# The second normalised tiles of block 0: turned by VectorE through DRAM in place of TensorE

## The chip, the cores and the metric

One core of a Trainium2 chip runs the kernel alone. The metric is the device time of one execution in microseconds, the median of repeated runs. The profile is of one further execution on the same kind of core.

## The reference

A transformer block whose two normalisations are scaled and shifted by a condition c. `x` has 2048 rows of 512, `wqkv` is 512 x 1536, the inner width F is 1792, and there are 32 heads of 16.

```python
mod = (_silu(c) @ w_mod).reshape(c.shape[0], 6, 1, -1)
h = _layernorm(x) * (1 + ca) + sa
# attention without softmax: phi(t) = where(t > 0, t + 1, exp(t)) + 1e-6
kv = einsum("bhsd,bhse->bhde", phi(k), v);  z = einsum("bhsd->bhd", phi(k))
o = einsum("bhqd,bhde->bhqe", phi(q), kv) / (einsum("bhqd,bhd->bhq", phi(q), z) + 1e-6)
x = x + ga * (o @ wo)
h = _layernorm(x) * (1 + cb) + sb
x = x + gb * (mish(h @ w1 + b1) @ w2)
```

All of it is float32.

## The kernel before

The 2048 rows are four blocks (b) of 512, a block is four row tiles (t) of 128, and a row of 512 is four column tiles (j) of 128. Every matmul operand is split into a high and a low part (`split`: ScalarE copies the high part, VectorE subtracts it to get the low one), and a product is three matmuls (`mm3`: L76, L77, L78).

The work has stages. First keys and the sums over all rows; then queries, by `q_unit(b, g)` and `q_sevens`; then the output of attention, by `o_unit(b, t)`, twelve matmuls each; then the two dense layers, first for the blocks 0 and 1 and then for 2 and 3. The first dense layer takes two blocks at a time by a seven-product scheme (`pair_begin`, `pair_early`, ..., `product` L1142): its operands are, for each pair of blocks, the second normalised tiles turned so that the 512 columns lie on partitions (`hf`, split as b11, b12, b21, b22) and sums of them (`columns`, t1 to t4).

The order of the instructions is written out by hand. A unit of matmuls is issued in the program's text; what follows it on other engines is a generator given to `spawn`. `tick()` advances every running generator by one `yield`, so a generator's step stands between two units of matmuls, and "one tick earlier" means behind the unit before. `spawn_idle` puts a generator in a list of which the first two are advanced by each tick. Each engine runs its own instructions in order; so do the DMA queues of SP and POOL with the issuing of transfers. SBUF tiles come from one pool of 101 equal buffers (`SLOTS`), PSUM from three pools: "acc" with 4 banks, "h" with 3, "tp" with 1.

The steps around the change are these.

- `attend(b, wait, queue)`: TensorE's denominators `den` of block b (L893), VectorE's reciprocal `rden` (L897, L898), a store of it to DRAM (L900) and four loads that broadcast it to the 16 rows of each head (`rd`, L904), all on the given queue; then, `wait` ticks later, VectorE multiplies the four q tiles by it (L912), and they are split into `qs`, which `o_unit` reads. Block 2 and block 3 use SP.
- `o_post` (L924): VectorE adds the residual to an o unit's PSUM, giving `r`; for the blocks 2 and 3 POOL stores it (`x1d`, L929).
- `norm_first(t)` and `norm_each(b, t)`: mean and variance of a row tile of block 0 or block 1 by two ScalarE passes (`act_sums`) or by VectorE (`ln_stats`), the root by POOL (L207), and the normalised tile `n` by ScalarE (L216).
- `transpose_f(b, j)`: four TensorE transposes of the tiles of column j into one PSUM bank (`tp_n`, L997), and ScalarE scales and shifts them into `hf` (L999).
- `turn(...)`: another way to the same, used for block 3 of the first normalisation (`y_x`) and for the blocks 2 and 3 of the second. POOL stores the normalised row tiles to DRAM (`to_dram`, L247); `load_squares` loads each column tile in four transfers on SP (L262), so that 32 x 32 squares stand at the place of their mirror image; VectorE transposes inside the squares (L267), and ScalarE scales and shifts (L269).
- `w2_job(f)`: scales a tile of w2 (L719), splits it and stores it three times (L729, L731). `rows(g, wait)` loads w1 tiles (`w1p`, L786) and forms their sums and splits (`early_rows` are the first two); `store_rows` stores those (L818).

The lists in the loop at the end of attention give the unit behind which each column tile is turned:

```python
order = {8: [(0, 0), (0, 2)], 9: [(0, 1)], 10: [(0, 3), (1, 0)], 11: [(1, 2)], 12: [(1, 1)], 13: [(1, 3)]}
```

Of the kernel before, what the change touches and what calls it, by code (L numbers as in the profile page):

```python
# [27 lines left out]
def block_kernel(ctx: ExitStack, tc: tile.TileContext, x, wqkv, wo, w1, b1t, w2, c, wmodt, out):  # L28
# [23 lines left out]
    def spawn(gen):  # L52
        fresh.append(iter(gen))

    def spawn_idle(gen):

        idle_work.append(gen)

    def tick():

        running.extend(fresh)
        fresh.clear()
        for g in list(running):
            if next(g, "end") == "end":
                running.remove(g)
        for g in idle_work[:width[0]]:
            if next(g, "end") == "end":
                idle_work.remove(g)
# [145 lines left out]
    def ln_apply(key, b, j, t, dst, engine):  # L214
        if engine is act:
            act.activation(dst, t, AF.Identity, bias=nb[key, b][:, j:j + 1], scale=rs[key, b][:, j:j + 1])  # L216
        else:
            engine.tensor_scalar(dst, t, mv[key, b][:, j, 0:1], rs[key, b][:, j:j + 1],
                                 op0=ALU.subtract, op1=ALU.mult)
# [143 lines left out]
    def q_unit(b, g):  # L363
        p = ps("h", f"pq_{b}_{g}")
        gs = slice(P * g, P * (g + 1))
        for k in range(4):
            mm3(p, [w[:, gs] for w in wq[k]], hT["x", b, k], k == 0, k == 3)
        pq[b, g] = sb(f"q_{b}_{g}")
        spawn(phi(p, f"q_{b}_{g}", pq[b, g]))
# [342 lines left out]
    def w2_job(f, wait=2):  # L712
        if f not in w2r:
            load_w2(f)
        if f > 1:
            for _ in range(wait):
                yield
        t = w2r[f]
        dve.tensor_tensor(t, t, bc["gb"], op=ALU.mult)  # L719
        yield  # L720
        yield from split(f"w2_{f}", t, w2s, f)
        yield
        g, n = f // 2, f % 2
        if n == 0:
            w2f[g] = drp.tile([P, 2, D], F32, name=f"w2f_{g}")
            for i in range(2):
                w2d[g, i] = drp.tile([P, 2, D], F32R, name=f"w2d_{g}_{i}")
        for i in range(2):
            pool.dma_start(w2d[g, i][:, n, :], w2s[f][i])  # L729
        if g < KEPT:  # L730
            pool.dma_start(w2f[g][:, n, :], t)  # L731
# [49 lines left out]
    def rows(g, wait):  # L781

        r = [sb(f"w1p_{g}_{i}", F32, (P, 4, P)) for i in range(2)]
        for i in range(2):
            f = 2 * g + i
            sp.dma_start(r[i], w1[:, P * f:P * (f + 1)].rearrange("(k p) f -> p k f", p=P))  # L786
        for _ in range(wait):
            yield
        a11, a12, a21, a22 = [r[i][:, 2 * k:2 * k + 2, :] for i in range(2) for k in range(2)]
        s12, s34 = [sb(f"s{n}_{g}", F32, (P, 4, P)) for n in (12, 34)]  # L790
        s1, s2, s3, s4 = s12[:, 0:2, :], s12[:, 2:4, :], s34[:, 0:2, :], s34[:, 2:4, :]
        dve.tensor_tensor(s1, a21, a22, op=ALU.add)
        dve.tensor_tensor(s2, s1, a11, op=ALU.subtract)
        dve.tensor_tensor(s3, a11, a21, op=ALU.subtract)
        dve.tensor_tensor(s4, a12, s2, op=ALU.subtract)
        yield
        keep, todo = {}, []
        op_rows[g] = keep
        for name, v, parts in (("a1", r[0], ("a11", "a12")), ("s12", s12, ("s1", "s2")), ("s34", s34, ("s3", "s4")),
                               ("a22", a22, ("a22",))):  # L800
            half = split(f"{name}_{g}", v, keep, name)
            next(half)
            todo.append((name, half, parts))
            if len(todo) == 2:
                yield
                for name, half, parts in todo:
                    run(half)
                    for i, part in enumerate(parts):
                        op_a[g, part] = [h[:, 2 * i:2 * i + 2, :] for h in keep[name]]
                todo = []  # L810
# [19 lines left out]
    early_rows = [rows(g, 3 * g + 1) for g in range(2)]  # L830
# [54 lines left out]
            tick()  # L885


    def attend(b, wait, queue=pool):

        p = ps("tp", f"den_{b}")[:, 0:P]  # L890
        for g in range(4):
            for t in range(4):
                pe.matmul(p[32 * t:32 * (t + 1), :], hmask[:, g, :], pq[b, g][:, P * t:P * (t + 1)],  # L893
                          start=g == 0, stop=g == 3)
        yield
        rden = cst.tile([P, P], F32, tag="rden", name=f"rden_{b}", bufs=2)
        dve.tensor_scalar(rden, p, tiny_den[:, 0:1], 1.0, op0=ALU.add, op1=ALU.mult)  # L897
        dve.reciprocal(rden, rden)  # L898
        d = drp.tile([32, 512], F32, name=f"rden_d_{b}")
        queue.dma_start(bass.AP(tensor=d.tensor, offset=d.offset, ap=[[P, 4], [512, 32], [1, P]]), rden)  # L900
        rd = []
        for g in range(4):
            r = sb(f"rd_{b}_{g}")
            queue.dma_start(r, bass.AP(tensor=d.tensor, offset=d.offset + 8 * g * 512,  # L904
                                     ap=[[512, 8], [0, 16], [1, 512]]))
            rd.append(r)
        for _ in range(wait):
            yield
        parts = []
        for g in range(4):  # L910
            t = pq[b, g]
            dve.scalar_tensor_tensor(t, t, TINY, rd[g], op0=ALU.add, op1=ALU.mult)  # L912
            parts.append(split(f"qs_{b}_{g}", t, qs, (b, g)))
            next(parts[-1])
            if g % 2:
                yield
                run(parts.pop(0))
                run(parts.pop(0))
# [18 lines left out]

    def norm_first(t):

        yield  # L940
        sums = act_sums("n", 0, t, xt["r", 0, t])
        yield
        sums_eps("n", 0, t, sums)
        yield
        sums_shift("n", 0, t, sums)
        yield
        v = xt["n", 0, t] = sb(f"n_0_{t}")
        ln_apply("n", 0, t, xt["r", 0, t], v, act)

    def norm_each(b, t):  # L950

        if t < 2:
            yield
            sums = act_sums("n", b, t, xt["r", b, t])
            yield
            sums_eps("n", b, t, sums)
            yield
            sums_shift("n", b, t, sums)
        else:
            ln_stats("n", b, t, xt["r", b, t])  # L960
            ln_eps("n", b, t, t + 1)
            ln_rstd("n", b, t, t + 1)
            yield
            ln_shift("n", b, t, t + 1)
        v = xt["n", b, t] = sb(f"n_{b}_{t}")
        ln_apply("n", b, t, xt["r", b, t], v, act)
# [27 lines left out]
    def transpose_f(b, j, ptag="tp"):  # L994
        p = ps(ptag, f"tp_n_{b}_{j}")
        for t in range(4):
            pe.transpose(p[:, P * t:P * (t + 1)], xt["n", b, t][:, P * j:P * (j + 1)], ident)  # L997
        hf[b, j] = sb(f"hf_n_{b}_{j}")
        act.activation(hf[b, j], p, AF.Identity, bias=mc[:, 12 + j:13 + j], scale=mc[:, 16 + j:17 + j])  # L999

    def split_b(b, j, name):
        return split(f"{name}_{b}_{j}", hf[b, j], op_b, (name, j % 2))
# [65 lines left out]
        tick()  # L1068
    for g in range(4):
        q_unit(3, g)  # L1070
        tick()
        if g == 1:
            spawn_idle(early_rows[1])
            for t in range(4):
                o_unit(0, t)
                spawn(norm_first(t))
                if t == 1:
                    spawn(attend(2, 5, sp))
                tick()
    act.preload_act_table_set("mish")  # L1080

    order = {8: [(0, 0), (0, 2)], 9: [(0, 1)], 10: [(0, 3), (1, 0)], 11: [(1, 2)], 12: [(1, 1)], 13: [(1, 3)]}
    for b in range(1, NB):
        for t in range(4):
            n = 4 * b + t
            for i, j in order.get(n, ()):
                transpose_f(i, j, "h")
                spawn(split_b(i, j, f"b{j // 2 + 1}{i + 1}"))
            if n in (12, 13):
                spawn(columns(0, n - 12, ("b11", "b12", "b21", "b22")))  # L1090
            if n == 14:
                break
            o_unit(b, t)
            if b == 1:
                spawn(norm_each(1, t))
            if n == 4:
                load_w2(0)
                load_w2(1)
            if n == 5:
                spawn(attend(3, 3, sp))  # L1100
            if n == 7:
                spawn(w2_job(0))
                spawn(w2_job(1))
            tick()


# [163 lines left out]
    for t in (2, 3):  # L1270
        if t == 3:
            spawn(rows(2, 3))
        o_unit(NB - 1, t)
        tick()
    tiles = [norm_tile(b, t) for b in (2, 3) for t in range(4)]
# [279 lines left out]
```

## Time and profile before

| | |
|---|---|
| median of 3 runs | 484.92 us (484.68 to 484.94) |
| profiled execution | 484.99 us, of which the span is 483.0 us |
| instructions | 7291 |
| TensorE, VectorE, ScalarE, POOL busy | 477.7, 384.5, 295.7, 148.4 us |
| granted TensorE clock | 1.00 |
| moved by DMA | 101.69 MB, mean 211 GB/s |

The span is the time from the first to the last instruction in the trace. In the lines that follow, PE is TensorE's matmuls, PEld its weight loads, DVE VectorE, ACT ScalarE, POOL GpSimd and SP the engine that only issues DMAs (SPq). A line of a timeline has its start in us from the start of the span, its length in us, the engine, the line of the kernel, the operation, the tiles written and read, the shape, how many instructions are merged in it and, in brackets, how long the engine stood idle before and what ended that.

### The profile page before, as it was taken

To read this page: it belongs to the slowest core of one execution; us is meant where nothing else is said; L and a number is where in the kernel's file an instruction comes from. 1 tells how busy PE (TensorE), PEld (TensorE's weight loads), DVE (VectorE), ACT (ScalarE), POOL (GpSimd) and SP (SyncE) were. 2 spreads that over 40 slices of the span, in tenths; PEclk is the share of its full clock that TensorE was granted. 3 is DMA by queue.
4 is the path that set the end of the run, shared out by engine and by line. 5 is a ranking of instruction groups with operands and counts; after the bars stand their busy time and mean duration, and the time that the engine had idled before them with its cause. 6 is when DMAs were issued, how large, how long until landed. Compare 5 with 4: busy or idle time off the path is not lost.

```text
span 483.0 us, 7291 instructions
## 1 busy us (share of the span) xinstructions
PE 477.7 (99%) x2342; PEld 393.6 (81%) x2342; DVE 384.5 (80%) x741; ACT 295.7 (61%) x528; POOL 148.4 (31%) x248
## 2 busy tenths in 40 slices
PE   8999999999999999999999999999999999999997
PEld 6788887878878888888888888888888888888887
DVE  7989989999799699977775874899644664789993
ACT  6777686866555979647676755683174454668300
POOL 4583320000022114102324434323617410243500
PEclk9999999999999999999999999999999999999999
DMA  8805599144874307389699998979999922499977
GB/s 312 299 9 127 138 160 266 51 135 150 290 196 110 121 30 263 111 284 335 216 299 350 364 251 187 321 227 340 346 363 332 291 61 62 109 181 211 240 117 167
DMA packets 121823, 101.69 MB, mean 211 GB/s; under 512 B 65937, under 2 KB 87449, under 8 KB 121786
## 3 DMA queue, kind: packets, MB, share of 16 engines
q1 hardware_dynamic: 90504, 55.47, 41.2%
q0 software_dynamic: 29024, 45.24, 37.3%
q10 hardware_dynamic: 2258, 0.53, 0.5%
q8 instruction: 18, 0.29, 0.3%
q14 instruction: 19, 0.16, 0.1%
HBM read 64.50 MB, written 34.61 MB: 205 GB/s over the span
## 4 chain that ended last, share of the span: by engine, by line
PE 93%; DVE 4%; ACT 1%; issue 1%; POOL 0%; ACTq 0%; DVEq 0%
PE p_a L1142 20%; PE p_s L1142 8%; PE oacc L78 5%; PE oacc L76 5%; PE oacc L77 5%; PE m L78 5%; PE m L77 5%; PE m L76 5%; PE o L76 3%; PE o L78 3%; PE o L77 3%; PE pq_a L409 3%; PE pk L78 2%; PE pk L76 2%; PE pk L77 2%; PE gacc L77 2%
## 5 line engine op out<-in xcount | busy, mean ns | idle before, releaser
L207 POOL TENSOR_TENSOR rs_n<-rs_n,half 128x1 f32<-128x1 f32 x16 | 11.4, 711 | 62.0 <-DVE rs_n L202 36.4
L1147 DVE TENSOR_TENSOR cb<-p_s,u 128x512 f32<-128x512 f32 x28 | 19.2, 687 | 11.6 <-ACT u L1183 10.9
L1152 ACT ACTIVATE u<-p_a 128x512 f32<-128x512 f32 x14 | 8.4, 598 | 26.2 <-PE p_a L1142 17.9
L1440 POOL DMA_DIRECT2D wt_m<-w2t x20 | 14.0, 702 | 32.9 <-PE p_a L1142 21.4
L1134 ACT ACTIVATE ub<-cb,b1c 128x512 f32<-128x512 f32 x28 | 20.0, 717 | 5.6 <-DVE cb L1147 5.4
L1177 ACT ACTIVATE u<-p_a 128x512 f32<-128x512 f32 x12 | 7.2, 599 | 24.7 <-PE p_a L1142 24.7
L1183 ACT ACTIVATE u<-p_a 128x512 f32<-128x512 f32 x14 | 8.4, 597 | 15.7 <-PE p_a L1142 15.7
L1147 DVE TENSOR_TENSOR c<-p_a,u 128x512 f32<-128x512 f32 x14 | 9.5, 688 | 8.2 <-PE p_a L1142 7.1
L900 POOL DMA_DIRECT2D rden_d<-rden x2 | 1.4, 719 | 46.5 <-DVE rden L898 46.5
L300 ACT ACTIVATE e_k<-pk 128x512 f32<-128x512 f32 x15 | 8.9, 591 | 10.8 <-PE pk L78 10.8
L779 POOL DMA_DIRECT2D w2b<-w2d x20 | 10.6, 541 | 14.5 <-DVE r L1126 4.6
L773 POOL DMA_DIRECT2D wb<-w2d x14 | 9.9, 709 | 12.4 <-DVE t L751 10.7
L303 DVE SCALAR_TENSOR_TENSOR ku<-e_k,relu_k 128x512 f32<-128x512 f32 x15 | 10.7, 713 | 3.1 <-ACT relu_k L301 3.1
L1111 ACT ACTIVATE u<-p_a,b1c 128x512 f32<-128x512 f32 x14 | 9.6, 684 | 5.4 <-PE p_a L1142 5.4
L303 DVE SCALAR_TENSOR_TENSOR q<-e_q,relu_q 128x512 f32<-128x512 f32 x16 | 10.7, 687 | 2.7 <-ACT relu_q L301 2.7
L207 POOL TENSOR_TENSOR rs_x<-rs_x,half 128x1 f32<-128x1 f32 (+1 forms) x10 | 7.7, 780 | 15.8 <-DVE rs_x L202 14.6
L312 POOL DMA_DIRECT2D ku<-ku x8 | 7.2, 898 | 16.5 <-DVE ku L303 16.5
L826 POOL DMA_DIRECT2D a1b<-rd_a x10 | 5.4, 540 | 21.1 <-DVE b_1l L90 9.6
L924 DVE TENSOR_TENSOR r<-o,r 128x512 f32<-128x512 f32 x16 | 10.9, 680 | 0.9 <-PE o L78 0.9
L719 DVE TENSOR_TENSOR w2r<-w2r,gb_bc 128x512 f32<-128x512 f32 x14 | 9.1, 686 | 2.7 <-DMA w2r<-in_w_dram 2.7
L912 DVE SCALAR_TENSOR_TENSOR q<-q,rd 128x512 f32<-128x512 f32 x16 | 10.5, 689 | 0.5 <-DMA rd<-rden_d 0.5
L929 POOL DMA_DIRECT2D x1d<-r x8 | 4.4, 546 | 20.9 <-DVE r L924 20.9
(1617 smaller groups left out, 1892.6 us busy)
## 6 DMA issues: line engine op xcount, KB each, us to landing
wm<-in_wmodt_dram SPq DMA_DIRECT2D x24, 256.0 KB, 5.4
w2b<-w2d POOLq DMA_DIRECT2D x20, 256.0 KB, 6.3
wt_m<-w2t POOLq DMA_DIRECT2D x20, 256.0 KB, 6.0
r<-in_x_dram SPq DMA_DIRECT2D x16, 256.0 KB, 3.5
x<-in_x_dram SPq DMA_DIRECT2D x15, 256.0 KB, 4.8
w1p<-in_w_dram SPq DMA_DIRECT2D x14, 256.0 KB, 4.1
w2r<-in_w_dram SPq DMA_DIRECT2D x14, 256.0 KB, 6.2
wb<-w2d POOLq DMA_DIRECT2D x14, 256.0 KB, 5.4
```

What stands on the lines that cost most here:

```text
L76: pe.matmul(o, st[0], mv[0], start=start, stop=False)
L77: pe.matmul(o, st[0], mv[1], start=False, stop=False)
L78: pe.matmul(o, st[1], mv[0], start=False, stop=stop)
L207: pool.tensor_tensor(y, y, half[:, lo:hi], op=ALU.pow)
L303: dve.scalar_tensor_tensor(dst, e, 1.0, r, op0=ALU.min, op1=ALU.add)
L409: pe.matmul(p, l, r, start=onto is None and c == 0 and i == 0, stop=c == 1 and i == 2, skip_group_check=onto is not None)
L779: pool.dma_start(w2s[f][i], w2d[f // 2, i][:, f % 2, :])
L924: dve.tensor_tensor(r, p, r, op=ALU.add)
L1134: act.activation(u, p, AF.Mish, bias=b1c[:, f:f + 1])
L1142: pe.matmul(p, st, mv, start=onto is None and c == 0 and i == 0, stop=c == 1 and i == 2, skip_group_check=onto is not None)
L1147: dve.tensor_tensor(out, p, u, op=ALU.add)
L1440: pool.dma_start(v, w2t[g][:, :, SUM[name], :])
```

## The change

Block 0's second normalised tiles go the way of `turn`: each of the four row tiles is stored to DRAM, the column tiles are loaded in sixteen transfers, transposed by VectorE and scaled by ScalarE. TensorE's sixteen transposes of block 0 are gone; block 1's stay. Around that, steps move:

- `norm_first` of the last row tile begins one tick earlier, and the sums of the second pair of w1 tiles are begun one tick earlier.
- `attend(2)` waits four ticks in place of five. `attend(3)` is spawned one unit earlier and waits one tick more.
- The squares of the column tiles 0 and 2 are loaded before unit 5; those of 1 and 3 between the store of block 3's `rden` and the loads of `rd`, on the same queue.
- `order` changes: block 0's splits come one unit or so later, block 1's column tiles 0 and 2 are transposed together behind the same unit.
- In block 1, the row tile 2 takes its statistics from ScalarE.
- The first two `w2_job` go from unit 7 to the last o unit of block 3, behind the first products of the dense layer.

```diff
-    def attend(b, wait, queue=pool):
+    def attend(b, wait, queue=pool, between=None):
...
         queue.dma_start(bass.AP(tensor=d.tensor, offset=d.offset, ap=[[P, 4], [512, 32], [1, P]]), rden)
+        if between is not None:
+            between()
...
     def norm_first(t):
 
-        yield
+        if t < 3:
+            yield
...
         ln_apply("n", 0, t, xt["r", 0, t], v, act)
+        to_dram("n", 0, t, v)
 
     def norm_each(b, t):
 
-        if t < 2:
-            yield
+        if t != 3:
+            if t < 2:
+                yield
             sums = act_sums("n", b, t, xt["r", b, t])
...
     for g in range(4):
         q_unit(3, g)
-        tick()
         if g == 1:
             spawn_idle(early_rows[1])
+        tick()
+        if g == 1:
             for t in range(4):
                 o_unit(0, t)
                 spawn(norm_first(t))
                 if t == 1:
-                    spawn(attend(2, 5, sp))
+                    spawn(attend(2, 4, sp))
                 tick()
...
-    order = {8: [(0, 0), (0, 2)], 9: [(0, 1)], 10: [(0, 3), (1, 0)], 11: [(1, 2)], 12: [(1, 1)], 13: [(1, 3)]}
+    turns = {7: (0,), 8: (2,), 9: (1, 3)}
+    order = {9: [(0, 0)], 10: [(0, 2), (0, 1)], 11: [(0, 3), (1, 0), (1, 2)], 12: [(1, 1)], 13: [(1, 3)]}
     for b in range(1, NB):
         for t in range(4):
             n = 4 * b + t
             for i, j in order.get(n, ()):
-                transpose_f(i, j, "h")
+                if i:
+                    transpose_f(i, j, "h")
                 spawn(split_b(i, j, f"b{j // 2 + 1}{i + 1}"))
+            if n == 5:
+                load_squares("n", 0, (0, 2))
+            for j in turns.get(n, ()):
+                spawn(turn_f(0, j))
...
-            if n == 5:
-                spawn(attend(3, 3, sp))
-            if n == 7:
-                spawn(w2_job(0))
-                spawn(w2_job(1))
+            if n == 4:
+                spawn(attend(3, 4, sp, lambda: load_squares("n", 0, (1, 3))))
             tick()
...
     for t in (2, 3):
         if t == 3:
             spawn(rows(2, 3))
+            spawn(w2_job(0))
+            spawn(w2_job(1))
         o_unit(NB - 1, t)
         tick()
```

More of the change, by code (lines that the diff above doesn't have):

```diff
@@ L1070, in block_kernel @@
         q_unit(3, g)
+        if g == 1:
+            spawn_idle(early_rows[1])
         tick()
         if g == 1:
-            spawn_idle(early_rows[1])
             for t in range(4):
```

## The prediction

> **What bounds the kernel now.** I read the page first: its busy line and its chain of work that ended last.
>
> ```profile
> span 483.0 us, 7291 instructions
> ...
> PE 477.7 (99%) x2342; PEld 393.6 (81%) x2342; DVE 384.5 (80%) x741; ACT 295.7 (61%) x528; POOL 148.4 (31%) x248
> ...
> PE 93%; DVE 4%; ACT 1%; issue 1%; POOL 0%; ACTq 0%; DVEq 0%
> ```
>
> TensorE is busy for 99% and carries 93% of the chain. So a microsecond taken out of TensorE's stream is worth a microsecond, and a microsecond for which TensorE is made to wait is lost at the end, since nothing behind it has slack. Next I read the windows around the change (columns: length, then busy time of PE, PEld, DVE, ACT, POOL, the granted clock, the DMA share and GB/s).
>
> ```profile
> 176.00:183.00 7.00, 7.00 (x38) 5.89 (x38) 6.79 (x19) 4.50 (x9) 2.43 (x3) 1.00 0.23 80
> 183.00:190.00 7.00, 7.00 (x38) 5.88 (x38) 6.82 (x12) 7.00 (x13) 4.32 (x8) 1.00 0.88 299
> 190.00:197.40 7.40, 7.40 (x39) 6.10 (x38) 7.37 (x13) 6.95 (x12) 1.08 (x2) 1.00 0.40 149
> 210.00:222.00 12.00, 12.00 (x55) 9.94 (x54) 7.67 (x15) 6.37 (x12) 0.73 (x2) 1.00 1.00 359
> ```
>
> TensorE never waits here, but VectorE is as full: 6.79 of 7.00, 6.82 of 7.00, 7.37 of 7.40 us. Anything that makes VectorE stand still in this stretch is passed on. At 210 to 222 us the DMA engines are full as well (share 1.00, 359 GB/s).
>
> **What the removed transposes are worth.** The timeline of TensorE at two groups of them (start, length):
>
> ```profile
> 177.40 1.03 PE L997 MATMUL tp_n<-ident,n 128*128 128x128 f32 x8
> ...
> 178.51 0.40 PE L77 MATMUL o<-m_0l,qs_0h 128*128 128x512 f32 x1
> 178.74 0.39 PE L78 MATMUL o<-m_0h,qs_0l 128*128 128x512 f32 x1
> ...
> 191.35 0.48 PE L76 MATMUL o<-m_0h,qs_0h 128*128 128x512 f32 x1
> ...
> 194.21 0.60 PE L997 MATMUL tp_n<-ident,n 128*128 128x128 f32 x4
> ```
>
> Matmuls follow each other every 0.23 us (178.51 to 178.74). From the first transpose to the second matmul behind it pass 178.51 - 177.40 = 1.11 us, where one matmul alone would take 0.23: 0.88 us for 8 transposes, 0.11 each. Block 0 has 16 of them, so the change takes 16 x 0.11 = 1.76 us out of TensorE. ScalarE's four evictions stay as four activations of the same size; the sixteen 128-row pieces are replaced by four DMAs to DRAM, sixteen square loads and four VectorE transposes.
>
> Here a rule differs from the row. The Trainium skill, page "TensorE: Matmul & The Clock Gate", section "Part 4: PE-mode transpose", gives about 275 ns for one transpose in a kernel's context. By that the removal would be worth an estimated 4.4 us and the forecast below would read 486.0 instead of 488.6. The trace has eight overlapped ones in 1.03 us and a step of 0.11, so the measurement decides.
>
> **What VectorE gets.** Four transposes, and it loses the two multiplies and two subtractions of the first two w2 jobs, which go to a later stretch, and one set of statistics.
>
> ```profile
> 71.80 1.30 DVE L267 STREAM_TRANSPOSE hf_x<-y_x 128x512 f32<-128x512 f32 x2
> ...
> 187.79 0.68 DVE L90 TENSOR_TENSOR qs_0l<-q,qs_0h 128x512 fp32r<-128x512 f32 x1
> 188.39 0.69 DVE L90 TENSOR_TENSOR qs_1l<-q,qs_1h 128x512 fp32r<-128x512 f32 x1
> ```
>
> A transpose takes a step of 1.30/2 = 0.65 us, an elementwise operation 0.60 (187.79 to 188.39). Four of the first (2.6) against four of the second (2.4): nothing in sum. What matters is where VectorE must wait.
>
> **The new queue on SP.** In the kernel before, the reciprocal denominators of block 3 go out and come back through SP alone: one store, then four broadcast loads. In the changed kernel the order on SP is: eight square loads (tiles 0 and 2), the store, eight square loads (tiles 1 and 3), then the four broadcasts. Every square reads columns of all four row tiles, so the first waits for the landing of the last tile's write, and behind that wait stand the store and the broadcasts.
>
> ```profile
> 62.13 9.32 SPq L262 DMA_DIRECT2D y_x<-xd  x16
> ...
> 176.58 0.57 SPq L900 DMA_DIRECT2D rden_d<-rden  x1
> 179.09 2.57 SPq L904 DMA_DIRECT2D rd<-rden_d  x4
> ...
> 184.11 0.69 DVE L912 SCALAR_TENSOR_TENSOR q<-q,rd 128x512 f32<-128x512 f32 x1 [0.18 <-DMA rd<-rden_d]
> ...
> 165.98 0.59 ACT L301 ACTIVATE relu_q<-pq 128x512 f32<-128x512 f32 x1
> 166.45 0.63 ACT L84 ACTIVATE a_1h<-w1p 128x512 fp32r<-128x512 f32 x1
> ...
> 167.62 1.28 ACT L1080 ACT_TABLE_LOAD   x1
> ...
> 171.87 0.80 ACT L216 ACTIVATE n<-r,nb_n,rs_n 128x512 f32<-128x512 f32 x1
> 172.57 0.62 ACT L228 ACTIVATE scrap_n<-r 128x512 f32<-128x512 f32 x1
> ...
> 188.43 1.43 ACT L999 ACTIVATE hf_n<-tp_n,mc 128x512 f32<-128x512 f32 x2
> 189.75 0.63 ACT L84 ACTIVATE qs_2h<-q 128x512 fp32r<-128x512 f32 x1
> 190.31 0.63 ACT L84 ACTIVATE qs_3h<-q 128x512 fp32r<-128x512 f32 x1
> ```
>
> When does the last row tile exist? On ScalarE the new order behind relu_q (165.98, done with its step at 166.45) is two splits, the table load, two splits of q, then the row tiles 2 and 3. In the rows two full-width splits lie between 166.45 and 167.62, 1.17 us; in the new pair the second is half as wide, so I take 0.9. Then 1.28 for the table, 2 x 0.56 for the q splits (189.75 to 190.31), 0.70 for tile 2 (171.87 to 172.57) and 0.80 for tile 3: 171.2. Its write then has to land:
>
> ```profile
> L929 POOL DMA_DIRECT2D x1d<-r x8: 539/539/594, 183.6 to 211.3; - x8
> ...
> DMA to landing us min/median/max: 2.3/2.8/4.3
> ```
>
> With the quiet end of that row, 2.3 us, for a write of the same size and queue: 173.5 (with 4.3, 175.5). Eight squares at 9.32/16 = 0.58 us: 178.2. Store, 0.6: 178.8. Eight more squares: 183.5. So the first broadcast is issued at 183.5 instead of 179.09, 4.4 us later, though the store itself is ready early (its matmuls come one unit sooner, see below). In the kernel before the second broadcast ended a wait of VectorE at 184.11; 4.4 us later is 188.5.
>
> VectorE in the new order: q1 at 188.5 (step 0.60), two transposes (1.30), r, then qs_0l from 191.0 to 191.7, qs_1l to 192.3, q2, q3 (to 193.5), one b_0l, r, qs_2l to 195.3, qs_3l to 195.9. TensorE would start o(3,0) at 191.35 - 1.76 + 0.2 = 189.8. Its third matmul needs qs_0l: it arrives at 190.35 and waits until 191.7, 1.35 us. The seventh needs ScalarE's qs_2h (q2 done 192.9, plus 0.6): 0.9 us of waiting. The ninth needs qs_2l at 195.3: 1.35 us. Together 3.6 us, where the kernel before waited for nothing.
>
> Next late is the fourth group of block 1's transposes, tile 3. It takes the PSUM bank ("h", three of them) of the first group, which ScalarE must have evicted. In the new order that eviction (0.7, from the pair at 188.43) stands behind qs_2h and qs_3h (to 194.1), two scalings of turned tiles (2 x 0.7) and two splits (2 x 0.56): 196.6 to 197.3, while TensorE is there at 196.2. Another 1.1 us.
>
> **The earlier denominators.** The den matmuls of block 3 move from behind the second o unit of block 1 to behind the first, and VectorE's last phi of q_3, which they read, now stands behind two products that wait for block 2's broadcasts. Queued behind the wait on TensorE is all its later work.
>
> ```profile
> 161.15 2.64 SPq L904 DMA_DIRECT2D rd<-rden_d  x4
> ...
> 166.60 0.69 DVE L303 SCALAR_TENSOR_TENSOR q<-e_q,relu_q 128x512 f32<-128x512 f32 x1 [1.84 <-ACT relu_q L301]
> ...
> 170.81 1.08 PE L893 MATMUL den<-q,hmask 128*32 128x128 f32 x32
> ```
>
> TensorE would come to them one unit (twelve steps of 0.23, 2.7 us) sooner, at 168.1, and to the last four of them a quarter of a microsecond later. Block 2's second broadcast is issued at 161.8 (161.15 plus a quarter of 2.64), and with the 4.4 us that block 3's took (179.73 to 184.11) it lands at 166.2; q1 and q_3 behind it need 0.60 + 0.69, which is 167.5, or 168.5 where ScalarE's splits in front of them are late. I take 0.2 us; the bounds are 0 (as at 166.60 in the row) and 1.5 (the writes of row tiles 0 and 1, 0.52 MB at 359 GB/s, travel first). The o units that exchange places with den cost the same in either place: nothing.
>
> **The later w2 jobs.** The two jobs leave four VectorE operations, two ScalarE ones and six POOL writes of 256 KB to the stretch after 205 us.
>
> ```profile
> 209.26 1.00 SPq L786 DMA_DIRECT2D w1p<-in_w_dram  x2
> 210.31 0.50 SPq L818 DMA_DIRECT2D rd_a<-a_0h  x1
> ...
> 221.47 0.91 SPq L710 DMA_DIRECT2D w2r<-in_w_dram  x2
> ...
> 214.55 0.69 DVE L1147 TENSOR_TENSOR cb<-p_s,u 128x512 f32<-128x512 f32 x1 [3.51 <-ACT u L1183]
> ...
> 232.60 1.29 DVE L719 TENSOR_TENSOR w2r<-w2r,gb_bc 128x512 f32<-128x512 f32 x2
> ...
> L710 SPq DMA_DIRECT2D w2r<-in_w_dram x14: 328/406/1268, 163.8 to 277.3; - x14
> ...
> DMA to landing us min/median/max: 3.3/5.5/7.5
> ```
>
> In the changed program the buffers come round differently: the second w1p load of row pair 3 waits for the add cb of L1147, which in the trace starts at 214.55, plus the 3.1 us by which all is late by now, plus its 0.69: 218.3 instead of 209.8. Behind it on SP stand sixteen stores (210.31 to 221.47, 11.2 us) and the w2r loads: 229.5, and up to 4.4 us later if the six extra writes (1.57 MB at 359 GB/s) go first. The multiply that reads them is due at 232.60 + 3.1 = 235.7. Landing 3.3 to 5.5 us after the issue gives 232.8 to 239.4, so VectorE waits 0 to 3.7 us, of which TensorE sees what VectorE's own idle time behind it (3.5 us at 214.55, for one) does not take. I take 0.5, bounds 0 and 2.5.
>
> **Sum.** The profiled execution took 484.99 us, 1.99 around its span of 483.0, against a median of 484.92: the same. 484.99 - 1.76 + 0.2 + 3.6 + 1.1 + 0.5 = 488.63, so 488.6.
>
> **Rivals.**
> - *No stall, faster.* If the squares went out at the pace of their quickest issue and the broadcasts landed as before, TensorE would keep only the gain: 484.99 - 1.76 + 0.2 = 483.4. It decides at the second broadcast's landing: at 187.1 or sooner TensorE's first wait is gone, and the others shrink by as much.
>
> ```profile
> L262 SPq DMA_DIRECT2D y_x<-xd x16: 333/487/957, 62.1 to 71.0; - x16
> ```
>
> For it: the quickest issue is 333 ns. Against it: the median is 487 and the whole took 9.32 us; sixteen at 0.33 would save 4.0 us, just what is needed. Chance 0.13, and 0.04 more for a partial stall that ends within 0.2% of before.
> - *Late w2 loads as well.* The chain through the w1p buffer takes its whole 3.7 us and little of it is covered: another 2 to 3 us, 491. For it: the DMA share of 1.00 at 210 to 222 us. Against it: VectorE's idle times. Chance 0.2.
> - *Slow squares.* Each square costs 0.15 us more than the mean of the sixteen (they reach 957 ns in the row): 16 x 0.15 = 2.4 us on the path to the broadcasts, 491.0. For it: they now share the DMA engines with the writes of block 0 and 2. Against it: the sixteen of the row had a full window too. Chance 0.03. The Trainium skill, page "DMA: Bandwidth & Descriptors", section "Specifications", speaks for this one: it wants 512 B or more per transfer for the full rate, and these rows are of 128 B; at a quarter of its 358 GB/s, 1 MB would take an estimated 11.7 us. The trace disagrees by its 9.32 us for the same sixteen.
> - *Dear transposes.* Were each worth its own length (0.60 for four that step by 0.11, so 0.27) and not the step, 16 x 0.16 = 2.6 us less, 486.0. Against it: the steps of these very instructions. Chance 0.02.
>
> **How the numbers follow.** Forecast 0.58, no stall 0.13, partial 0.04, late loads too 0.20, slow squares 0.03, dear transposes 0.02. A measurement of this kernel tells 0.2%, about 1 us, from no change. Slower 0.83, same 0.04, faster 0.13. The forecast's own bounds: squares at the median of 487 ns (16 x 0.09 = 1.4 us) and no w2 wait (0.5) take it down to 486.7, a write that lands in 4.3 us up to 490.6. The range leaves out the fast rival and the far end of the late one: 485.2 to 491.2.
>
> **What would show it.** Right: 16 fewer transposes; VectorE idle for some 4 us before a q product at L914, ended by a broadcast's DMA; TensorE waits in o(3,0) for qs of VectorE and ScalarE, and at the last tp_n group for ScalarE; w1p and the stores on SP some 8 us later. Wrong: TensorE without waits between 185 and 200 us, or a first broadcast issued before 181.

## The result, and the profile after

The changed kernel takes 492.75 us (median of six runs, 492.12 to 493.28) beside 484.85 us of the kernel before (six runs, 484.64 to 484.94): the ratio is 1.0164, interval 1.0151 to 1.0177. It is slower, as forecast, but by 7.9 us where 3.7 were forecast, and 492.75 lies above the range's end of 491.2. The profiled execution took 493.25 us.

The page of the kernel after, its busy line and its chain of work that ended last:

```profile
span 491.5 us, 7306 instructions
...
PE 481.5 (98%) x2326; PEld 393.9 (80%) x2326; DVE 386.2 (79%) x743; ACT 297.4 (61%) x532; POOL 149.8 (30%) x252
...
PE 83%; DVE 8%; DMA 3%; ACT 2%; issue 1%; SPq 1%; POOL 1%; ACTq 0%; DVEq 0%
```

The sixteen transposes are gone (2342 to 2326 matmul instructions), yet TensorE is busy for 3.8 us more. Its share of the last chain fell from 93% to 83%; VectorE and the DMA engines took it. The windows of the kernel after (columns as in the prediction: length, busy PE, PEld, DVE, ACT, POOL, granted clock, DMA share, GB/s) say where:

```profile
183.00:190.00 7.00, 7.00 (x38) 5.69 (x37) 0.69 (x1) 1.40 (x3) 0.58 (x1) 1.00 0.71 175
190.00:200.00 10.00, 6.31 (x15) 3.64 (x16) 9.05 (x15) 6.82 (x12) 1.08 (x2) 0.66 0.28 94
200.00:210.00 10.00, 10.00 (x40) 8.18 (x39) 9.38 (x17) 6.95 (x14) 1.35 (x3) 0.83 0.28 88
```

VectorE does 0.69 us of work in 7 us (183 to 190), where it did 6.82. Then TensorE is idle for 3.7 of 10 us, and the granted clock is 0.66 and 0.83. That is why TensorE's busy time grew: the same matmuls took longer. The timelines of the kernel after, of SP's issuing and then of VectorE:

```profile
174.40 4.04 SPq L262 DMA_DIRECT2D y_n<-nd  x8
178.54 0.58 SPq L900 DMA_DIRECT2D rden_d<-rden  x1
179.22 5.19 SPq L262 DMA_DIRECT2D y_n<-nd  x8
184.51 2.57 SPq L906 DMA_DIRECT2D rd<-rden_d  x4
```

```profile
188.55 0.69 DVE L914 SCALAR_TENSOR_TENSOR q<-q,rd 128x512 f32<-128x512 f32 x1 [5.69 <-DMA rd<-rden_d]
190.73 0.69 DVE L914 SCALAR_TENSOR_TENSOR q<-q,rd 128x512 f32<-128x512 f32 x1 [1.49 <-DMA rd<-rden_d]
191.34 1.30 DVE L267 STREAM_TRANSPOSE hf_n<-y_n 128x512 f32<-128x512 f32 x2
...
193.13 0.67 DVE L90 TENSOR_TENSOR qs_0l<-q,qs_0h 128x512 fp32r<-128x512 f32 x1
```

And TensorE, first in the kernel before and then in the kernel after, at the second, third and ninth matmul of o(3,0) and at the first product of the dense layer (in brackets the idle time and what ended it):

```profile
191.67 0.40 PE L77 MATMUL o<-m_0l,qs_0h 128*128 128x512 f32 x1
191.90 0.40 PE L78 MATMUL o<-m_0h,qs_0l 128*128 128x512 f32 x1
...
193.29 0.40 PE L78 MATMUL o<-m_2h,qs_2l 128*128 128x512 f32 x1
...
197.40 0.39 PE L1142 MATMUL p_a<-b_0h,a_0h 128*128 128x512 f32 x1
```

```profile
190.29 0.40 PE L77 MATMUL o<-m_0l,qs_0h 128*128 128x512 f32 x1
193.86 0.79 PE L78 MATMUL o<-m_0h,qs_0l 128*128 128x512 f32 x1 [3.17 <-DVE qs_0l L90]
194.45 0.63 PE L76 MATMUL o<-m_1h,qs_1h 128*128 128x512 f32 x1
...
197.46 0.80 PE L78 MATMUL o<-m_2h,qs_2l 128*128 128x512 f32 x1 [0.52 <-DVE qs_2l L90]
...
203.34 0.43 PE L77 MATMUL o<-m_2l,qs_2h 128*128 128x512 f32 x1
...
204.52 0.39 PE L1152 MATMUL p_a<-b_0h,a_0h 128*128 128x512 f32 x1
```

The difference of the starts is the running account. TensorE comes to o(3,0) 1.38 us ahead (190.29 against 191.67). At the third matmul it is 1.96 behind: the step there took 3.57 us instead of 0.23. At the ninth it is 4.17 behind, at p_a 7.12. Between 193.86 and 203.34 neighbouring matmuls start about 0.43 us apart where they had 0.23. The span ends 8.5 later, so another 1.4 is lost behind p_a.

### The profile page after: what moved, and what is told of

Same layout as the page of the kernel before. It is cut to its first block, busy times and chain, and to the rows that moved or that the text cites. A ratio compares the mean times of both kernels' runs of the same rounds, so it can differ in the third digit from the quotient of the medians.

```text
span 491.5 us, 7306 instructions
## 1 busy us (share of the span) xinstructions
PE 481.5 (98%) x2326; PEld 393.9 (80%) x2326; DVE 386.2 (79%) x743; ACT 297.4 (61%) x532; POOL 149.8 (30%) x252
## 4 chain that ended last, share of the span: by engine, by line
PE 83%; DVE 8%; DMA 3%; ACT 2%; issue 1%; SPq 1%; POOL 1%; ACTq 0%; DVEq 0%
PE p_a L1152 19%; PE p_s L1152 8%; PE oacc L76 5%; PE oacc L78 5%; PE oacc L77 5%; PE m L77 5%; PE m L76 5%; PE m L78 5%; PE pq_a L409 3%; PE pk L76 2%; PE pk L78 2%; PE pk L77 2%; PE gacc L77 2%; PE gacc L78 2%; PE gacc L76 2%; PE o L78 2%
## 5 line engine op out<-in xcount | busy, mean ns | idle before, releaser
L914 DVE SCALAR_TENSOR_TENSOR q<-q,rd 128x512 f32<-128x512 f32 x16 | 10.4, 683 | 7.2 <-DMA rd<-rden_d 7.2
L826 POOL DMA_DIRECT2D a1b<-rd_a x10 | 5.4, 540 | 24.3 <-PE p_a L1152 11.1
L269 ACT ACTIVATE hf_n<-hf_n,mc 128x512 f32<-128x512 f32 x12 | 9.3, 804 | 4.3 <-DVE hf_n L267 4.3
```

## The experiments

The theory after the result (A): the late broadcasts make TensorE wait for over 3 us, the wait lowers its clock, and both cost time. The rivals are named in the expectations. The first four kernels of the table ran on one chip beside the kernel before, and so did the next four, the four after them, and the last. From group to group the kernel before varies by 0.3 us.

| kernel | median us | before us | ratio, interval |
|---|---|---|---|
| fill14 | 494.56 | 484.90 | 1.0202 (1.0187 to 1.0217) |
| rd_first | 495.45 | 484.90 | 1.0224 (1.0203 to 1.0245) |
| rd_pool | 492.82 | 484.90 | 1.0164 (1.0149 to 1.0180) |
| w2_back | 491.69 | 484.90 | 1.0151 (1.0132 to 1.0170) |
| fill14_w2 | 491.76 | 485.14 | 1.0139 (1.0099 to 1.0180) |
| fill14_early | 495.70 | 485.14 | 1.0208 (1.0172 to 1.0244) |
| turn11 | 490.07 | 485.14 | 1.0095 (1.0066 to 1.0124) |
| turn11_w2 | 493.37 | 485.14 | 1.0158 (1.0139 to 1.0177) |
| before_late8 | 490.24 | 485.12 | 1.0111 (1.0079 to 1.0143) |
| before_late16 | 494.41 | 485.12 | 1.0204 (1.0178 to 1.0230) |
| order4 | 486.86 | 485.12 | 1.0039 (1.0024 to 1.0054) |
| order4_mid | 486.03 | 485.12 | 1.0015 (1.0002 to 1.0029) |
| order4_mid13 | 485.40 | 485.04 | 1.000 (0.999 to 1.001) |

### fill14: TensorE kept busy during the wait

```diff
+                fill = ps("tp", "fill")
+                for _ in range(14):        # between the second and the third matmul of o(3,0)
+                    pe.matmul(fill, q[0], ms[g][0], start=True, stop=True)
```

> The changed kernel with 14 extra matmuls into a PSUM bank that nobody reads, put between the second and the third matmul of o(3,0), where TensorE stood still for 3.3 us (14 x 0.23 = 3.2 us). Theory A (standing still for over 3 us is what lowered the granted clock to 0.66): the third matmul still starts at about 193.9, but it and those behind it step by 0.23 instead of 0.43; the ninth waits for qs_2l until 197.4 all the same, and behind it 16 steps and four transposes take 4.1 us instead of 7.1: 2.9 us less, 489.8. Rival B (the clock falls from load or from the broadcasts, not from the wait): the drop is still there, 492.7, within 0.5.

Timeline of TensorE in this kernel, and its window:

```profile
190.11 3.36 PE L943 MATMUL fill<-m_0h,qs_0h 128*128 128x512 f32 x14
...
196.38 0.50 PE L78 MATMUL o<-m_2h,qs_2l 128*128 128x512 f32 x1 [1.01 <-DVE qs_2l L90]
198.36 0.66 PE L1011 MATMUL tp_n<-ident,n 128*128 128x128 f32 x4 [0.79 <-ACT hf_n L1013]
201.60 0.39 PE L1161 MATMUL p_a<-b_0h,a_0h 128*128 128x512 f32 x1
...
246.02 0.50 PE L1161 MATMUL p_s<-b_2h,s_2h 128*128 128x512 f32 x1 [2.93 <-DVE cb L1166]
```

```profile
190.00:200.00 10.00, 7.93 (x35) 5.67 (x34) 9.30 (x16) 7.90 (x14) 1.62 (x3) 1.00 0.22 83
```

With TensorE busy through the stall the clock stays at 1.00 here, so in this stretch it was the standing still that lowered it, and not the load or the broadcasts (rival B). Two later kernels with the same 14 matmuls limit this; they follow below. From the ninth matmul to p_a pass 5.22 us instead of 7.06; by these two profiled executions the low clock cost 1.84. It is not 2.9, because at full clock TensorE meets the wait that the prediction had at the last tp_n group (0.79 and the slower restart). The other 1.08 by which p_a is sooner came from broadcasts that happened to land sooner. And yet the number was missed, and the whole is 1.8 us slower than the changed kernel: everything won is lost again at 246 us, and more, at a wait of 2.93 us for cb (the longest for cb in the changed kernel is 0.7). A second chain ends there.

### rd_first and rd_pool: the broadcasts sooner

```diff
# rd_first                                   # rd_pool
-        if between is not None:             -  spawn(attend(3, 4, sp, lambda: ...))
-            between()                       +  spawn(attend(3, 4, pool, lambda: ...))
         rd = []
...
             rd.append(r)
+        if between is not None:
+            between()
```

> The changed kernel with the four broadcast loads of block 3 ahead of the second eight square loads on SP instead of behind them. Theory A (the broadcasts were late because of the queue): first broadcast issued at about 179.2, its q product at 183 to 184; the transposes of tiles 1 and 3 then wait for their squares (to about 189), qs_0l at 191, TensorE waits 0.5 us at the third matmul of o(3,0) and about 2 at the ninth, the clock stays at 1.00: 487.4 (485.5 to 489). Rival C (the four transposes and VectorE's order are what is late, whatever the broadcasts do): the wait at the third matmul stays over 3 us and the time is 492 or more.

> The changed kernel with block 3's store of the denominators and its four broadcasts on POOL's queue, the sixteen squares alone on SP. Theory A: broadcasts issued at about 176.5 and landed by 182, squares landed by 186.3, qs_0l at 189.2, no wait at the third matmul, 0.9 us at the ninth, clock 1.00: the first product p_a of the last stage starts 0.5 us sooner than in the kernel before, and with the 1.2 us lost to the later w2 jobs the time is 485.5 (484 to 487). Rival C (transposes and VectorE's order): 491 or more. Rival D (POOL's queue delivers the broadcasts no sooner than SP's): 490 to 493, with q products again at 188 or later.

The timelines of SP and of VectorE in rd_first, and then the same two of rd_pool:

```profile
180.98 2.55 SPq L904 DMA_DIRECT2D rd<-rden_d  x4
183.58 8.16 SPq L262 DMA_DIRECT2D y_n<-nd  x8
```

```profile
186.50 0.69 DVE L914 SCALAR_TENSOR_TENSOR q<-q,rd 128x512 f32<-128x512 f32 x1 [1.08 <-DMA rd<-rden_d]
192.30 0.71 DVE L267 STREAM_TRANSPOSE hf_n<-y_n 128x512 f32<-128x512 f32 x1 [5.10 <-DMA y_n<-nd]
```

```profile
175.70 13.93 SPq L262 DMA_DIRECT2D y_n<-nd  x16
```

```profile
190.60 0.71 DVE L267 STREAM_TRANSPOSE hf_n<-y_n 128x512 f32<-128x512 f32 x1 [2.51 <-DMA y_n<-nd]
```

Both missed their numbers (487.4 and 485.5) and lie where rival C put them (492 or more, 491 or more). The second q product came 4.2 us sooner in rd_first and 3.3 in rd_pool, but now VectorE waits for squares, and TensorE waits 5.25 and 1.89 us for qs_0l. Behind the broadcasts eight squares take 8.16 us to issue, 1.02 each, where the first eight of the changed kernel took 4.04; beside the broadcasts of the other queue sixteen take 13.93. Whichever goes first, the other is late, and VectorE's order asks for both before qs_0l. So the trade is not on SP's queue alone: broadcasts in flight slow the squares. Rival C is right that VectorE's order of transposes matters, but what makes it late is the squares, and not the transposes' own time.

### w2_back, fill14_w2, fill14_early: the second chain

```diff
# w2_back, and with the 14 matmuls fill14_w2    # fill14_early (with the 14 matmuls)
+            if n == 7:                          +            load_w2(4)
+                spawn(w2_job(0))                +            load_w2(5)
+                spawn(w2_job(1))                             store_rows(0)
...
     for t in (2, 3):
         if t == 3:
             spawn(rows(2, 3))
-            spawn(w2_job(0))
-            spawn(w2_job(1))
```

> The changed kernel with the first two w2 jobs back behind unit 7, where the kernel before has them. Theory A (the later w2 jobs cost 0.4 and 0.8 us at two products behind 210 us): 1.2 us less, 491.5; the wait in o(3,0) is unchanged, since the four VectorE operations fall into the 5.7 us in which VectorE waits for the broadcast. Rival E (their six writes travel with the broadcasts and make them later, as the prediction's order of costs did not say): the wait in o(3,0) grows by 1 us or more and the time is 493 to 495.

> The 14 extra matmuls and the first two w2 jobs back behind unit 7. Theory F (two chains end close together: the stall in o(3,0), and the late loads w2r of jobs 4 and 5, which stand on SP behind sixteen stores and a w1p load and are due near 242 us; whoever shortens the first alone waits for the second): with the w2 jobs early the loads are out by 230 and the wait of 2.9 us for cb at 246 with its own drop of the clock is gone, so 490.6 to 491.7, some 3 to 4 us less than with the 14 matmuls alone (494.56), and at most 1 us less than with the w2 jobs back alone (491.69), where the clock was low for 3.4 us only and beside a wait for qs_2l. Rival G (the extra matmuls themselves cost the time): 493 to 495.

> The 14 extra matmuls, the w2 jobs late as in the changed kernel, but the two loads w2r of jobs 4 and 5 put on SP ahead of the sixteen stores. Theory F: the loads land before 230, the wait of 2.9 us for cb at 246 and its drop of the clock (about 1.7 us) are gone: 489.9 (489 to 491), which is the 2.9 us less than the changed kernel that the 14 matmuls were to bring. Rival G (the extra matmuls themselves) or H (the six late writes slow something else): 493 to 495.

SP in the changed kernel, its VectorE at the multiply that needs the last loads, and then SP in w2_back:

```profile
217.87 4.90 SPq L786 DMA_DIRECT2D w1p<-in_w_dram  x2
222.82 0.56 SPq L818 DMA_DIRECT2D rd_a<-a_0h  x1
...
239.82 0.94 SPq L710 DMA_DIRECT2D w2r<-in_w_dram  x2
```

```profile
242.77 1.41 DVE L719 TENSOR_TENSOR w2r<-w2r,gb_bc 128x512 f32<-128x512 f32 x2 [2.97 <-DMA w2r<-in_w_dram]
```

```profile
229.93 2.09 SPq L710 DMA_DIRECT2D w2r<-in_w_dram  x2
```

With the w2 jobs late, SP stands 4.90 us at a w1p load for its buffer, the sixteen stores take 17.0 us (222.82 to 239.82) beside twelve writes of POOL (the late six at 220.5 to 223.7, the next six from 228.9), and the loads of jobs 4 and 5 go out at 239.8. With the jobs early they go out at 229.9, and behind p_a nothing more is lost: p_a starts at 203.78, 6.38 behind the kernel before, and the span of 489.4 ends 6.4 behind. The number came out (491.69 for 491.5), though not by the sum that gave it, for the stall itself is not unchanged: the third matmul of o(3,0) starts at 194.95 instead of 193.86. It is not rival E, since the second q product ran at 190.62, as before; two of the four VectorE operations (the splits w_0l and w_1l, 1.2 us) stand behind it and ahead of qs_0l, and not in the idle stretch as the expectation had it. The matmuls of w2_back are at full pace again by 198.56, and the low clock lay wholly beside the wait for qs_2l.

fill14_w2 loses 6.6 us against its kernel before where fill14 lost 9.7, so the loss of fill14 behind p_a was the late w2 chain and not the extra matmuls (G falls). But it is no faster than w2_back (491.76 and 491.69), and its clock fell after all, behind the stall (its window from 200 to 210 us):

```profile
200.00:210.00 10.00, 9.58 (x41) 7.94 (x41) 9.39 (x17) 7.81 (x14) 1.08 (x2) 0.87 0.14 54
```

Its matmuls are slow from 199.1 to 202.3 us, behind waits of 0.58, 0.66 and 1.01 us within 4.2 us. In fill14_early the same happens from 199.5 on (waits of 0.46, 1.01 and 0.79; clock 0.85 from 200 to 210), and in rd_pool at 196 (1.89 and 0.66; 0.77 from 190 to 200). So short waits close together can lower the clock too, and no pair of times shows the 1.84 us of the low clock as a gain of the whole kernel. fill14_early missed its number by 5.8 us: the loads of jobs 4 and 5 went out at 229.0, but those of jobs 6 and 7 at 254.1, VectorE waited 6.95 us for them and TensorE 3.9. Another place in the queue only hands the lateness on.

### turn11 and turn11_w2: the transposes behind qs_3l

```diff
+    # on top of rd_first; turn11_w2 with the w2 jobs at unit 7 as well
-    turns = {7: (0,), 8: (2,), 9: (1, 3)}
-    order = {9: [(0, 0)], 10: [(0, 2), (0, 1)], 11: [(0, 3), (1, 0), (1, 2)], 12: [(1, 1)], 13: [(1, 3)]}
+    turns = {7: (0,), 8: (2,), 11: (1, 3)}
+    order = {9: [(0, 0)], 10: [(0, 2)], 11: [(1, 0), (1, 2)], 12: [(0, 1), (0, 3), (1, 1)], 13: [(1, 3)]}
```

> The changed kernel with the broadcasts ahead of the second eight squares, and with the two VectorE transposes of tiles 1 and 3 two units later, behind qs_2l and qs_3l of block 3, their splits accordingly. Theory J (squares and broadcasts take from each other on the DMA engines, together some 10 us from 178.5 on, and either order leaves VectorE waiting because its order asks for both before qs_0l): with the transposes behind, qs_0l is there at 188, TensorE does not wait in o(3,0), the clock stays at 1.00 and the first product p_a starts at 196.0, 1.4 us sooner than in the kernel before; the late w2 loads then cost their 4 to 5.5 us at 230 to 250: 488.9 (487 to 490). Rival C (the transposes themselves, wherever they stand): 492 or more.

> As the run before it, and the first two w2 jobs back behind unit 7. Theory J with F: both chains are gone, 16 transposes of TensorE less and nothing waits: 483.5 (483 to 485), faster than both kernels. If the w2 jobs' six writes make the squares and broadcasts later by 2 us or more (rival E): 486 to 488.

TensorE in turn11:

```profile
193.44 0.50 PE L78 MATMUL o<-m_2h,qs_2l 128*128 128x512 f32 x1 [1.40 <-DVE qs_2l L90]
...
201.37 0.50 PE L1152 MATMUL p_a<-b_1l,a_0h 128*128 128x512 f32 x1 [2.63 <-DVE b_1l L90]
...
202.63 0.56 PE L1152 MATMUL p_a<-b_3h,a_0h 128*128 128x512 f32 x1
...
205.97 0.46 PE L1152 MATMUL p_a<-b_1h,a_1l 128*128 128x512 f32 x1
```

The wait for qs_0l is gone and turn11 is the first kernel below 491, but it came out 1.2 above its number, since the split b_1l now stood behind four differences of `columns` on VectorE and p_a waited for it. That it missed by no more is luck: 4.5 us are lost inside the first products, where none was forecast, and behind them the late w2 loads cost 0.5 and not 4 to 5.5. In turn11_w2 the six writes go out among the squares, whose last eight then take 9.58 us to issue; the wait at b_1l grows to 3.63, with one of 0.97 ahead of it. Rival E holds there, by more than its number.

### before_late8 and before_late16: late broadcasts in the kernel before

```diff
+        for i in range(2 if b == 3 else 0):     # 4 in before_late16
+            y = drp.tile([P, 512], F32, name=f"late_{i}")
+            for sq, rows_ in [*squares(y, nd["x", 3], P * (i % 4))]:
+                sp.dma_start(sq, rows_)
         rd = []
```

> The kernel before with eight extra square reads of 128-byte pieces (DRAM to DRAM, read by nobody) on SP between block 3's store of the denominators and its four broadcasts; nothing else changed. Theory A (late broadcasts alone make the loss): first broadcast issued 4 to 5 us later, second q product at 188.5 to 190.7 instead of 184.1, TensorE waits 1 to 3 us in o(3,0) for qs_0l and again for qs_2l; 488 to 490. Rival C (the loss needs the turned tiles): 485 to 486.

> The same with sixteen such reads. Theory A: second q product at 193 to 196, TensorE waits 4 to 7 us in o(3,0) and the granted clock falls behind it as in the changed kernel, where it fell behind 3.3 us: 493 to 497, with a granted clock of 0.6 to 0.9 in the 10 us after the wait. Rival B (the drop of the clock has to do with the changed kernel's own load): the time is longer by the wait alone and the clock stays 1.00.

The timelines of SP and of TensorE and a window of before_late8, and then the same three of before_late16:

```profile
184.06 2.63 SPq L908 DMA_DIRECT2D rd<-rden_d  x4
```

```profile
193.10 0.66 PE L1001 MATMUL tp_n<-ident,n 128*128 128x128 f32 x4 [1.34 <-ACT hf_n L1003]
```

```profile
190.00:200.00 10.00, 6.35 (x29) 4.09 (x28) 9.49 (x16) 6.54 (x12) 3.73 (x7) 1.00 0.73 242
```

```profile
189.24 2.63 SPq L908 DMA_DIRECT2D rd<-rden_d  x4
```

```profile
197.02 1.11 PE L1001 MATMUL tp_n<-ident,n 128*128 128x128 f32 x4 [5.94 <-ACT hf_n L1003]
```

```profile
190.00:200.00 10.00, 4.06 (x14) 2.84 (x13) 6.26 (x11) 3.15 (x6) 3.19 (x6) 0.70 0.63 206
```

Without a single turned tile, broadcasts issued 5 us later make the kernel 5 us slower, and 10 us later make it 9.3 slower. The first has four waits of at most 1.34 us and a clock of 1.00; the second has one of 5.94, one of 0.91 and a clock of 0.70. Theory A holds on both counts: lateness alone makes the loss, and a long wait lowers the clock without the changed kernel's load. The wait came at another place than said: TensorE stopped first at a tp_n group, whose PSUM bank ScalarE had not emptied because it stood before qs_0h for 6.6 us.

### order4, order4_mid, order4_mid13: both chains taken out

```diff
# order4, on top of turn11's two lists
     def attend(b, wait, queue=pool, between=None):
...
         if between is not None:
-            between()
+            between[0]()                        # squares of tiles 0 and 2
         rd = []
...
             rd.append(r)
+        if between is not None:
+            between[1]()                        # squares of tiles 1 and 3
...
-            if n == 5:
-                load_squares("n", 0, (0, 2))
...
-            if n in (12, 13):
-                spawn(columns(0, n - 12, ("b11", "b12", "b21", "b22")))
+            if n == 13:
+                for c in range(2):
+                    spawn(columns(0, c, ("b11", "b12", "b21", "b22")))
# order4_mid: the two w2 jobs are spawned at n == 12, order4_mid13: at n == 13, ahead of columns
```

> The changed kernel with SP's order store, squares of tiles 0 and 2, broadcasts, squares of tiles 1 and 3 (the store goes out 4 us sooner and nothing on SP stands still for its landing), the VectorE transposes of tiles 1 and 3 behind qs_3l, and the differences of the first column pair one unit later so that the splits of tiles 1 and 3 stand ahead of them. w2 jobs late as in the changed kernel. Theory J: squares landed by 191.5, broadcasts by 187, no wait in o(3,0) nor at p_a, clock 1.00 to 235 us; the late w2 loads then cost 4 to 5.5 us: 488.5 (487 to 490). If the squares beside the broadcasts still take 1 us each and more, b_1l is late by up to 2 us: 490 to 492.

> As the run before it, with the first two w2 jobs spawned ahead of unit 13 of the o units, two steps of TensorE sooner than in the changed kernel: their six writes go out at 204 to 208, behind the squares and ahead of the sixteen stores. Theory F with J: both chains gone, 16 transposes less on TensorE: 484.0 (483.3 to 485.5), the fastest of all. If the writes still run into the stores: 486 to 488.

> As the last kernel, with the two w2 jobs one unit later, so that their two multiplies on VectorE stand behind the splits of tiles 1 and 3. Theory K (nothing is left but the wait of 1.3 us for b_1l that the two multiplies made, and behind it the gain of the removed transposes shows): b_1l ends at 197 instead of 198.4, TensorE waits 0.3 to 0.5 us there, 0.8 to 1.3 us less than 486.03: 484.9 (484.2 to 485.4), at or just below the kernel before. Rival L (the late chain of writes, stores and loads takes back what is won in front of it, as it did with the 14 matmuls): 486 or more, with a wait behind 210 us.

The waits of TensorE behind the start in order4, in order4_mid and in order4_mid13 (total, times, longest):

```profile
PE p_s L1153 <- DVE cb L1158: 2.8, 2, 2.0
...
PE p_a L1153 <- ACT u L1194: 0.6, 1, 0.6
```

```profile
PE p_a L1156 <- DVE b_1l L90: 1.3, 1, 1.3
```

```profile
PE o L76 <- DVE r L928: 0.5, 1, 0.5
PE p_s L1155 <- DVE t_0l L90: 0.3, 1, 0.3
PE p_s L1155 <- DVE t_1l L90: 0.2, 1, 0.2
```

None of the three waits in o(3,0). order4 reaches p_a at 195.71, 1.69 ahead of the kernel before, and with the w2 jobs still late its span ends 3.1 behind. Of these 4.8 us, 3.4 are lost at the two waits for cb (240 and 271 us), which is the second chain; the other 1.4 are gone by 215 us. (The profiled execution took 487.82, 1.0 more than the median, so 3.4 may be high.) order4 came out 1.6 below its number. With the jobs in the middle the waits for cb are gone, but order4_mid gave 486.03 for 484.0. order4_mid13 was to give 484.9 and gave 485.40, the same as the kernel before. It starts p_a at 195.97, 1.43 ahead, and loses 2.0 by 215 us, half of it at the three waits above, all for VectorE. Neither K nor L: the wait for b_1l is gone and its chain of loads is in time, but VectorE, busy for 9.97 of the 10 us from 190 to 200 and 9.90 of the next 10 (two windows of order4_mid13), is behind when TensorE is ahead. It was as full in the kernel before (9.86 and 10.00 in the same windows), so TensorE had little to gain there:

```profile
190.00:200.00 10.00, 10.00 (x48) 8.24 (x47) 9.97 (x18) 8.43 (x15) 1.62 (x3) 1.00 0.34 100
200.00:210.00 10.00, 8.89 (x38) 6.41 (x37) 9.90 (x17) 8.33 (x15) 3.61 (x7) 1.00 0.42 112
```

## Why the prediction was wrong in size

The account of the profiled execution, from the starts above, beside the terms of the sum:

| step | predicted | measured |
|---|---|---|
| TensorE at o(3,0) | -1.56 (transposes -1.76, den 0.2) | -1.38 |
| first wait, qs_0l | 1.35 | 3.34 |
| up to the ninth matmul, qs_2h and qs_2l | 2.25 | 2.21 |
| last tp_n group, tile 3 | 1.1 | 1.1 (in fill14; here the slow matmuls cover it) |
| low clock up to p_a | no term | 1.84 (against fill14) |
| late w2 loads | 0.5 | 1.4 |
| sum | 3.64 | 8.5 |

**Right.** The sign and the mechanism: the broadcasts stand behind sixteen squares, VectorE stands still before a q product at L914 (5.69 us; some 4 were forecast), and TensorE waits for qs_0l and qs_2l. The transposes' 0.11 each is borne out: from 0.22 behind after den (172.38 for 172.16) TensorE gains 1.60 up to o(3,0), 0.10 for each of the sixteen. The first broadcast was forecast for 183.5 and issued at 184.51.

**Wrong, first wait.** The step that failed is "4.4 us later is 188.5" for the second q product: it ran at 190.73. One microsecond is the issue: the first square went out at 174.40 instead of 173.5, and the second eight took 5.19 instead of 4.66, of which the first eight gave back 0.6 (4.04). The other 1.2 is the transfer: issued at about 185.15, the second broadcast ended VectorE's wait 5.6 us later, not 4.4. The 4.4 came from a trace in which no squares travelled beside it. In the four later kernels with the same order on SP it took 4.7 to 5.2, so some of the 1.2 changes from execution to execution; that the squares make the rest is likely and not shown. Everything behind on VectorE moved by 2.2 as a block, so the wait rose from 1.35 to 3.34.

**Wrong, a missing term.** The sum knew waits and no clock, and behind the wait of 3.17 us it was low for 9.5 us. Whether the waits that the sum did forecast (1.35, 0.9, 1.35 and 1.1) would have left the clock alone is not settled: in before_late8 waits of 1.34, 0.64, 0.67 and 1.01 us did, in fill14_w2 smaller ones did not. The Trainium skill, page "TensorE: Matmul & The Clock Gate", section "HAM oscillation — how this bites in real kernels", asks for no idle gap of TensorE over some 3.4 us. These traces agree that such a gap halves the pace (0.43 for 0.23 us), and put the bound lower: gaps of 2.63 and 2.93 us were followed by it too, and so were shorter ones that came close together.

**Wrong, the rival's size.** The late w2 loads were given 0.5, bounds 0 and 2.5, and as a rival another 2 to 3. The chain was drawn rightly (buffer of w1p, sixteen stores, w2r), but it starts from an instruction of TensorE's stream, so it slid along with the stall: the w1p load came at 222.4 and not 218.3. The stores took 17.0 us, not 11.2. In the changed kernel most of that is hidden by the stall ahead of it; alone, it is worth some 3.4 (order4). The "no stall" rival (483.4) was no way out either: in order4, which has no stall and still the late w2 jobs, this chain held the time at 486.86. The two were set as cases side by side, where they are two chains of which mainly the later one counts.

What stays open: why the low clock lasted 9.5 us in the changed kernel, and some 3.4 us in turn11; and what decides whether waits below 2.6 us lower it, since neither the longest nor their sum does (2.01 us in order4, and 2.3 us in three waits within 4.3 us in before_late8, left it at 1.00).

## What to carry to other kernels

Before a step is moved to a queue, list what stands behind it there and who waits for that, and take transfer times from a trace in which the new neighbours travel too, or add for them. When a forecast has TensorE waiting for some 2 us within 4, in one piece or in several, add a term for the clock, with a chance of its own. When two late chains run side by side, price each alone and take the later one, and expect that a gain on the bounding engine will be met by the next engine that is full.

## What the runs showed of the hardware

- All eight gaps of 2.63 us and more in TensorE's stream were followed by matmuls at about half the pace. Behind 2.63 us (turn11) and 2.93 us (fill14, at 246 us) the clock fell some 1.3 and 0.8 us after work resumed, and stayed low for 3.4 us. Behind 3.17 us (the changed kernel) and 5.94 us (before_late16) the first matmuls were slow at once.
- Shorter gaps went both ways. Single ones of 1.31 (order4_mid), 1.40 (turn11) and 2.01 us (order4) left the clock alone, and so did 1.34, 0.64, 0.67 and 1.01 us in a row (before_late8) and 0.27, 1.01 and 0.79 us (fill14). Behind 1.89 and 0.66 us (rd_pool), 0.58, 0.66 and 1.01 us (fill14_w2) and 0.46, 1.01 and 0.79 us (fill14_early) it fell.
- Eight loads of squares, with rows of 128 bytes, issue at 0.50 us each with no broadcasts ahead of them (4.04 us in the changed kernel) and at 1.0 us each when four broadcasts of 256 KB were issued just ahead (8.16 us in rd_first).
- Sixteen stores took 15.6 to 18.2 us to issue when the first two w2 jobs' six writes of 256 KB went out beside them (the changed kernel, fill14, turn11, order4), and 11.1 to 13.4 us when those had gone out earlier (before, w2_back, order4_mid, order4_mid13).
